# The last stage of an attention, mixture and gate chain in two passes, with seven block products in place of eight

## The chip, the cores and the metric

The kernel runs on one core of one Trainium2 chip. The metric is the device time of one execution in microseconds, as the median of several runs. A core has five engines that matter here, each with a queue of its own that it works through in order: TensorE (PE, matrix products into PSUM, with its weight loads listed as PEld), VectorE (DVE), ScalarE (ACT), GpSimd (POOL), and SyncE (SP), which here issues every DMA. An instruction starts when those ahead of it on its engine have started and its semaphore waits are met.

## The reference, cut to what matters

Three stages follow each other, for four batches of 576 tokens: an attention with 8 heads, a mixing layer (`_moe_ref`) and a gated layer, in which all of the change lies:

```python
def _moe2_ref(x, w_in, w_spatial, b_spatial, w_out):
    h = np.maximum(x @ w_in, 0.0)                # x: 4 x 576 x 512, w_in: 512 x 1024
    u, v = (h[..., :512], h[..., 512:])
    mu = np.mean(v, axis=-1, keepdims=True)
    var = np.mean((v - mu) ** 2, axis=-1, keepdims=True)
    v_n = (v - mu) / np.sqrt(var + 1e-06)
    v_s = np.einsum('ts,bsd->btd', w_spatial, v_n) + b_spatial[None, :, None]
    return ((u * v_s) @ w_out)                   # w_spatial: 576 x 576, w_out: 512 x 512
```

## The kernel before, in words

Everything is float32 at the interface. A product of two float32 matrices is made of three matmuls: each operand is split into a rounded high half and the remaining low half (names ending in h and l, or `_0` and `_1`), and hi·hi, hi·lo and lo·hi are added in PSUM. A split is a cast and a subtraction (`halves`, line 1342).

The instruction order is not the order of the source. Every step is handed to a planner (class `Plan`, line 185) by `add`, with the engines that could do it and an estimated cost; `Plan.order` then emits one list, by a list schedule whose priorities are the step's due time `plan.at` plus numbers from the table `TUNE` (line 57), one row per tag and kind of step. Where the planner expects PE to be idle, it inserts small matmuls of a constant into `psT`, whose result nobody reads. Since all instructions go through one helper, the profile knows them by line L500 alone; they are told apart by the tiles that they write and read.

The last stage (`moe2`, line 1737) is one pass per batch. It splits the batch's `x` into `x2h` and `x2l` (8 pieces of 288 columns); makes `vt`, the right half of the hidden layer, with tokens on partitions (4 tiles of 128 tokens, 12 matmuls of 512 columns each, into `psB`; the last 64 tokens of two batches share one more tile); normalises it on DVE (`BATCH_NORM_STATS2`, `mv`), splits it into `vh` and `vl`; makes `u`, the left half, with features on partitions; then the spatial product `sp`, the gate and the product with `w_out`. The products `u` and `sp` are the ones that the change rewrites. Each has 8 groups per batch, 4 blocks of 128 features by 2 halves of 288 tokens. A `u` group contracts over 4 chunks of 128 with 3 matmuls each, 12; an `sp` group over 4 chunks of tokens with 3 each and a chunk of the last 64 tokens (`vx`, hi and lo stacked) with 2, 14. All of them are 288 columns wide and write the three banks `psM`. Then ACT takes `u` out of PSUM with the relu; for `sp` DVE adds the bias (`g<-psM,bb`), DVE or POOL multiplies by `u`, DVE or ACT casts to `gh` and DVE or POOL subtracts for `gl`. The `w_out` product and its copy `ot` end the batch; the batches' steps overlap as the planner's due times (1000 apart) allow.

Of the kernel before, what the change touches and what calls it, by code (L numbers as in the profile page):

```python
# [9 lines left out]
F32 = mybir.dt.float32  # L10
# [8 lines left out]
P = 128  # L19
# [18 lines left out]
def blocks(dil):  # L38
# [473 lines left out]
def kernel(  # L512
# [51 lines left out]

    enter("all", "cp")
    enter("all", "psM", space=PSUM)
    enter("one", "w1")
    enter("one", "mp")
    enter("att", "ap", side="right")
    enter("att", "psS", space=PSUM)  # L570
# [44 lines left out]
    def chunk(key, x):  # L615

        k = (key, x)
        if k not in tiles:
            home, tag = key, x
            if key[0] in WHOLE and x == 1:  # L620
                home, tag = before(key), 2
# [1422 lines left out]
```

## Time and profile before

| | us |
|---|---|
| median of 3 runs | 571.61 (570.77 to 572.67) |
| the profiled execution | 567.52 |
| its span in the trace | 565.7 |
| PE busy | 553.6 |
| DVE busy | 344.3 |
| ACT busy | 257.0 |
| POOL busy | 88.4 |

The profiled execution's own time is 4.1 us under the median and 1.8 us over its span. The profile lists for each engine the time in which it worked, and follows the chain of work that ended last back from the end, each step to what released it. The granted TensorE clock is 1.00 in every stretch, the higher of the two levels (2.4 GHz). The last stage runs from about 348 us to the end.

### The profile page before, as it was taken

How to read it: one execution, taken by the hardware profiler on the slowest of the kernel's cores; microseconds unless marked ns; L12 is line 12 of the kernel's file. 1: busy time of each engine (PE TensorE's matmuls, PEld its weight loads, DVE VectorE, ACT ScalarE, POOL GpSimd, SP SyncE). 2: the span in 40 equal slices, each digit the busy share in tenths (PEclk: the TensorE clock that was granted, in tenths of full speed). 3: DMA queues.
4: the chain of work that ended last, by engine and by line, in shares of the span. 5: the costliest groups of instructions: out<-in, count | busy, mean ns of one | idle time of the engine just before them, and what ended most of it. 6: DMA issues, size and time to landing. Idle time of an engine off the chain costs nothing.

```text
span 565.7 us, 13681 instructions
## 1 busy us (share of the span) xinstructions
PE 553.6 (98%) x5755; PEld 501.2 (89%) x5766; DVE 344.3 (61%) x782; ACT 257.0 (45%) x575; POOL 88.4 (16%) x105
## 2 busy tenths in 40 slices
PE   9999999998999999999999999999999999999997
PEld 5567876798999999999999999989889889988996
DVE  1999857957986383956689322389326428745150
ACT  2779825435724636316557560485334033214222
POOL 0100014432631022001001021006311000000030
PEclk9999999999999999999999999999999999999999
DMA  9978984357356200002342100312100010010002
GB/s 206 235 229 288 189 128 80 57 138 126 59 100 137 44 1 3 1 1 69 102 127 99 42 27 1 96 37 76 47 29 1 1 64 30 1 39 37 1 1 93
DMA packets 96253, 43.08 MB, mean 76 GB/s; under 512 B 81536, under 2 KB 89216, under 8 KB 96192
## 3 DMA queue, kind: packets, MB, share of 16 engines
q1 hardware_dynamic: 96192, 42.21, 31.7%
q8 instruction: 45, 0.74, 0.6%
q14 instruction: 16, 0.13, 0.1%
HBM read 37.47 MB, written 4.72 MB: 75 GB/s over the span
## 4 chain that ended last, share of the span: by engine, by line
PE 87%; DVE 3%; DMA 3%; ACT 2%; SPq 2%; issue 1%; DVEq 0%; ACTq 0%
PE psM L500 60%; PE psB L500 18%; PE psT L500 6%; SPq L500 2%; PE psS L500 2%; DMA room<-in_moe_w_v_dram 1%; DMA vw<-in_v_dram 1%; DVE xm L500 1%; DMA ld<-in_k_dram 1%; DVE xl L500 1%; ACT xh L500 0%; DVE xh L500 0%; ACT room L500 0%; ACT xm L500 0%; ACT wv L500 0%
## 5 line engine op out<-in xcount | busy, mean ns | idle before, releaser
L500 PE MATMUL psM<-xh,wk 128*128 128x288 f32 (+2 forms) x512 | 119.1, 326 | 1.5 <-DVE x L500 0.7
L500 PE MATMUL psM<-sq_dt.float32r,wv 128*128 128x288 f32 (+2 forms) x768 | 113.8, 299 | 1.0 <-ACT wv L500 0.6
L500 PEld LDWEIGHTS psM<-sq_dt.float32r,wv 128*128 128x128 f32 x768 | 104.5, 188 | 3.2 <-ACT wv L500 0.8
L500 PEld LDWEIGHTS psM<-xh,wk 128*128 128x128 f32 x512 | 87.1, 188 | 8.6 <-ACT xh L500 0.9
L500 PE MATMUL psM<-xh,wr 128*128 128x288 f32 (+2 forms) x256 | 64.0, 327 | 0.6 <-DVE xh L500 0.6
L500 PE MATMUL psM<-xl,wk 128*128 128x288 f32 x192 | 56.5, 295 | 0.1
L500 PE MATMUL psM<-x2h,wi 128*128 128x288 f32 x256 | 54.8, 296 | 0.0
L500 PEld LDWEIGHTS psM<-xh,wr 128*128 128x128 f32 x256 | 44.5, 188 | 3.9 <-DVE xh L500 0.7
L500 DVE TENSOR_TENSOR sq_dt.float32r<-kr,sq_dt.float32r 128x288 fp32r<-128x288 f32 (+2 forms) x54 | 26.8, 502 | 26.3 <-ACT sq_dt.float32r L500 25.8
L500 PEld LDWEIGHTS psM<-x2h,wi 128*128 128x128 f32 x256 | 42.2, 188 | 0.6 <-ACT u L500 0.2
L500 PE MATMUL psB<-wo,gh 128*128 128x512 f32 (+1 forms) x136 | 40.3, 379 | 0.0
L500 PE MATMUL psB<-wi,x2h 128*128 128x512 f32 x128 | 40.2, 395 | 0.0
L500 PE MATMUL psM<-x2l,wi 128*128 128x288 f32 x128 | 37.8, 296 | 0.9 <-DVE x2l L500 0.9
L500 ACT ACTIVATE kr<-psM 128x288 f32<-128x288 f32 (+2 forms) x50 | 20.3, 410 | 40.3 <-PE psM L500 37.0
L500 PE MATMUL psM<-wsh,vh 128*128 128x288 f32 x128 | 38.1, 298 | 0.0
L500 PE MATMUL psM<-wsl,vh 128*128 128x288 f32 x128 | 37.7, 295 | 0.0
L500 PE MATMUL psM<-wsh,vl 128*128 128x288 f32 x128 | 37.7, 294 | 0.0
L500 PEld LDWEIGHTS psM<-xl,wk 128*128 128x128 f32 x192 | 36.1, 188 | 0.3 <-DVE xl L500 0.3
L500 POOL TENSOR_TENSOR xl<-xm,xh 128x288 fp32r<-128x288 f32 x18 | 15.6, 876 | 127.6 <-ACT xh L500 67.8
L500 DVE BATCH_NORM_STATS2 bn<-vt 128x6 f32<-128x512 f32 x18 | 12.4, 691 | 37.6 <-ACT vt L500 37.5
L500 DVE TENSOR_TENSOR g<-psM,bb 128x288 f32<-128x288 f32 x32 | 14.3, 455 | 28.6 <-PE psM L500 25.1
L500 DVE SCALAR_TENSOR_TENSOR x<-x,psM 128x288 f32<-128x288 f32 (+2 forms) x32 | 14.3, 452 | 28.0 <-PE psM L500 27.8
(160 smaller groups left out, 1102.8 us busy)
## 6 DMA issues: line engine op xcount, KB each, us to landing
vw<-in_v_dram SPq DMA_DIRECT2D x36, 128.0 KB, 3.4
room<-in_moe_w_k_dram SPq DMA_DIRECT2D x8, 512.0 KB, 7.2
room<-in_moe_w_v_dram SPq DMA_DIRECT2D x8, 512.0 KB, 5.3
raw<-in_moe_w_in_dram SPq DMA_DIRECT2D x8, 512.0 KB, 3.8
ld<-in_q_dram SPq DMA_DIRECT2D x48, 72.0 KB, 2.6
ld<-in_k_dram SPq DMA_DIRECT2D x48, 72.0 KB, 2.7
vw<-in_v_dram SPq DMA_DIRECT2D x8, 288.0 KB, 5.3
room<-in_moe_w_r_dram SPq DMA_DIRECT2D x4, 512.0 KB, 4.2
```

The source lines that it names most:

```text
L500: return self.tc.keep_in_program_order(getattr(self.engine, name)(*args, **kw))
```

## The change

`moe2` is split in two functions. `first_half(b)` is run for all four batches, then `second_half(b)` for all four. Between them the normalised `vt` tiles lie in a DRAM tile `vnd` (16 DMAs of 256 KB to it, 8 of 512 KB back into the two `raw2` buffers, which the weight loads use before); `u` stays in SBUF, written over the batch's `x`, and is now kept without the relu, which moves into the gate (`SCALAR_TENSOR_TENSOR`, max with 0, then multiply).

The products `u` and `sp` are cut into 2 by 2 blocks and made from seven block products instead of eight (`seven`). A block product has two quarters `q` of 128 features and contracts over 2 chunks, so it is 2·2·3 = 12 matmuls of 288 columns, and seven of them 84. For `sp` 16 matmuls for the last 64 tokens are added. Some products need sums of blocks as operands: for `u` sums of `w_in` blocks, made once (`stationary`, tiles `qw`), and sums of `x` blocks, per batch (`moving`, tiles `t`); for `sp` sums of blocks of the transposed `w_spatial`, made once (`wsq`), and sums of blocks of the normalised `v`, per batch (`stationary` again, tiles `qv`). Products 1, 6, 7 and 4 accumulate one after another in the same bank of a quarter (`psM_91` and `psM_92`, "A"); in between, `take` copies the bank's value into a tile `sn` (for `sp` with the bias). Products 2, 5 and 3 use `psM_100` and a fifth bank of `psB` ("B"), and `final` adds an `sn` tile to a bank.

With this, per kernel, u and sp matmuls go from 832 to 736; transposes of `w_spatial` from 25 to 30 (6 blocks of 96 rows); DVE has 790 instructions for 732, ACT 605 for 565, POOL 139 for 100, and 270 DMAs are issued for 244. The whole table `TUNE` has new numbers, so all stages are ordered anew. The core of the diff:

```diff
...
-    ('u', 0): {'psM': (-2395, 121810, 792, 22), 'u': (73178, 190977, 792, 2000)},
...
+    ('T', 0): {'part3': (159936, 0, 792, 800), 'part1': (-65152, 0, 200, 800), 'part2': (-312122, 0, 1500, -300), 't': (-25768, 30350, 0, 0), 'part4': (68946, 0, 792, 2000)},
...
+    def quarter(i, x, phase):
+        k = 2 * (i - 1) + x
+        return held("w1", [P, 2, HD], F32R, f"q{phase}{k}", old_tags["wk"][k])
+
+    def hl(src, hi, lo, n, src_keys, hk, lk, after=()):
+
+        add(
+            {"act": act(n), "dve": dve2(n)}, lambda e: copy(e, hi(), src()),
+            r=src_keys, w=[hk], two="both", after=after,
+        )
+        return len(plan.ops) - 1, add(
+            {"dve": dve(n), "pool": pool(n)},
+            lambda e: two(e, lo(), src(), f32(hi()), ALU.subtract),
+            r=list(src_keys) + [hk], w=[lk], two=True,
+        )
+
+    def combine(o, a, b_, op, n, r, w, after=()):
+        return add(
+            {"dve": dve(n), "pool": pool(n)}, lambda e: two(e, o(), a(), b_(), op),
+            r=r, w=w, two=True, after=after,
+        )
...
+    def stationary(a11, a12, a21, a22, keys, phase, first=()):
+
+        k11, k12, k21, k22 = keys
+        QW = 2 * HD
+
+        def both(i, src, ks):
+            return hl(
+                src, quarter(i, 0, phase), quarter(i, 1, phase), QW, [*ks, *first], ("q", i, 0), ("q", i, 1),
+            )
+
+        both(1, a11, k11)
+        d12 = both(2, a12, k12)
+        x1 = combine(s_[0], a21, a22, ALU.add, QW, [*k21, *k22], [("vt", 0)])
+        combine(s_[1], s_[0], a11, ALU.subtract, QW, [("vt", 0), *k11], [("vt", 1)])
+        both(6, s_[1], [("vt", 1)])
+        both(5, s_[0], [("vt", 0)])
+        combine(a21, a11, a21, ALU.subtract, QW, [*k11, *k21], [("a21",)], after={x1})
+        both(7, a21, [("a21",)])
+        both(4, a22, k22)
+        combine(a12, a12, s_[1], ALU.subtract, QW, [*k12, ("vt", 1)], [("a12",)], after=d12)
+        both(3, a12, [("a12",)])
+        return [("a21",), ("a12",)]
+
+    ended = stationary(wq[0, 0], wq[0, 1], wq[1, 0], wq[1, 1], [wkept] * 4, "w", ["q room"])
...
+    def moving(b11, b12, b21, b22, keys, readers, split_, name):
+
+        k11, k12, k21, k22 = keys
+        QW = 2 * HALF
+        a3 = combine(b22, b22, b12, ALU.subtract, QW, [*k22, *k12], [(name, 3)], after=readers[3])
+        a1 = combine(b12, b12, b11, ALU.subtract, QW, [*k12, *k11], [(name, 1)], after={a3, *readers[1]})
+        combine(b11, b22, b11, ALU.add, QW, [(name, 3), *k11], [(name, 2)], after={a1, *readers[0]})
+        split_(6, b11, [(name, 2)])
+        split_(5, b12, [(name, 1)])
+        split_(7, b22, [(name, 3)])
+        combine(b21, b21, b11, ALU.subtract, QW, [(name, 2), *k21], [(name, 4)], after=readers[2])
+
...
+    def seven(name, b, at, left, right, tails, bias, final):
+
+            ps, key = bank_of(where, q)
+            n = 2 + (tail is not None)
+            for z in range(n):
+                last = z == n - 1
+
+                def emit(e, z=z, last=last):
+                    o = ps()[:, :HALF]
+                    fresh = start and z == 0
+                    flags = {} if start and stop else {"skip_group_check": True}
+                    if z == 2:
+                        nc.tensor.matmul(o, lh(), rh(), start=False, stop=False, **flags)
+                        nc.tensor.matmul(o, lh(), rl(), start=False, stop=True, **flags)
+                    nc.tensor.matmul(o, lh, rh, start=fresh, stop=False, **flags)
+                    nc.tensor.matmul(o, lh, rl, start=False, stop=False, **flags)
+                    nc.tensor.matmul(o, ll, rh, start=False, stop=last, **flags)
+
...
+        def take(ps, key, h):
+            t, tk = snap()
+            if bias is None:
+                add(
+                    {"act": actp(HALF), "dve": dve(HALF)}, lambda e: copy(e, t(), ps()[:, :HALF]),
+                    r=[key, "p2"], w=[tk],
+                )
+            else:
+                add(
+                    {"dve": dve(HALF)}, lambda e: two(e, t(), ps()[:, :HALF], bias(h), ALU.add),
+                    r=[key, "p2", "bb"], w=[tk],
+                )
+            return t, tk
+        qs = range(2)
+        for q in qs:
+            ps, key = run(1, q, "A")
+            t1 = take(ps, key, 0)
+            ps, key = run(2, q, "B", tail=tail(q, 0))
+            final(q, 0, ps, key, t1)
+        t2_, t3_, c_ = {}, {}, {}
+        for q in qs:
+            t2_[q] = take(*run(6, q, "A", False), 1)
+        right.late()
+        for q in qs:
+            c_[q] = run(5, q, "B")
+        for q in qs:
+            t3_[q] = take(*run(7, q, "A", False, tail=tail(q + 2, 1)), 1)
+            final(q + 2, 1, *c_[q], t3_[q])
+        for q in qs:
+            final(q + 2, 0, *run(4, q, "A", False, tail=tail(q + 2, 2)), None)
+        for q in qs:
+            final(q, 1, *run(3, q, "B", False, tail=tail(q, 1)), t2_[q])
+
...
+        def final(o, h, ps, key, t):
+            u = lambda: xs[b][:, o, h * HALF : (h + 1) * HALF]
+            area = users_of([(("T", b), ((2, 1), (4, 3))[o // 2][h])])
+            w = [("u", b, o, h)]
+            if t is None:
+                add({"act": actp(HALF), "dve": dve(HALF)}, lambda e: copy(e, u(), ps()[:, :HALF]), r=[key], w=w, after=area)
+            else:
+                add(
+                    {"dve": dve(HALF)}, lambda e: two(e, u(), ps()[:, :HALF], t[0](), ALU.add),
+                    r=[key, t[1]], w=w, after=area,
                 )
...
+    def second_half(b, base):
...
+        for j in range(2):
+            dma2(
+                packets(2 * P, 2048), vn[j],
+                lambda j=j: vnd[b, 2 * j * P : 2 * (j + 1) * P].rearrange("(a p) n -> p a n", p=P),
+                r=[("vnd", b, t) for t in (2 * j, 2 * j + 1)], w=[("vn", j), ("a21",) if j == 0 else ("a12",)],
+                after=raw_done,
+            )
...
+        def final(o, h, ps, key, t):
+            gk = plan.slot("g2", 6)
+            g = t2([P, HALF], F32, f"g{gk}", f"t{gk // 2}{gk % 2}")
+            hs = slice(h * HALF, (h + 1) * HALF)
+            add(
+                {"dve": dve(HALF)},
+                lambda e: two(e, g(), ps()[:, :HALF], t[0]() if t else bb()[:, hs], ALU.add),
+                r=[key, t[1] if t else "bb"], w=[("g2", gk)], after=t_done,
+            )
+            add(
+                {"dve": dve(HALF)},
+                lambda e: nc.vector.scalar_tensor_tensor(
+                    g(), xs[b][:, o, hs], 0.0, g(), op0=ALU.max, op1=ALU.mult
+                ),
+                r=[("g2", gk), ("u", b, o, h)], w=[("g2", gk)], two=True,
+            )
+            hl(
+                g, lambda: gh()[:, o, hs], lambda: gl()[:, o, hs], HALF,
+                [("g2", gk)], ("gh", o, h), ("gl", o, h), after=x_done,
...
     for b in range(B):
-        moe2(b, 10000 + 1000 * b)
+        first_half(b, 9200 + 600 * b)
+    for b in range(B):
+        second_half(b, 12000 + 600 * b)
```

Three places of the order. The first is ACT where the last stage begins, before: the gate inputs of the last mixing half (`x_1045`), then the eight casts of batch 0 into `x2h`.

```order
L500 ACTIVATE x_1045<-psM_92 128x288
L500 ACTIVATE x_1045<-psM_100 128x288
L500 ACTIVATE x_1045<-psM_91 128x288 x2
L500 CAST x2h<-x_120 128x288 x8
L500 ACTIVATE u<-psM_100 128x288
L500 ACTIVATE u<-psM_92 128x288
L500 ACTIVATE u<-psM_91 128x288
```

And now; `x_1053` is the last mixing half's tile, `wide` receives the transposed `w_spatial`.

```order
L558 ACTIVATE x_1053<-psM_91 128x288
L558 ACTIVATE wide<-psB_4191 128x4x96
L558 ACTIVATE wide<-psB_4284 128x4x96
L558 ACTIVATE wide<-psB_4365 128x4x96
L558 CAST x2h<-x_123 128x2x288 x3
L558 ACTIVATE wth<-psB_4365 128x96
L558 CAST wsq_0_4689<-wide 128x576
```

On ACT the casts were eight of 288 columns directly behind those of the mixing layer. Now there are three of 2x288, behind three copies for `wide`; the fourth is on DVE. DVE there before, with the last gate steps of the mixing layer:

```order
L500 SCALAR_TENSOR_TENSOR x_1045<-x_1045,psM_92 128x288
L500 SCALAR_TENSOR_TENSOR x_1045<-x_1045,psM_100 128x288
L500 SCALAR_TENSOR_TENSOR x_1045<-x_1045,psM_91 128x288
L500 SCALAR_TENSOR_TENSOR x_1045<-x_1045,psM_92 128x288
L500 MEMSET eps 128x1
L500 TENSOR_TENSOR x2l<-x_120,x2h 128x288 x2
L500 MEMSET zero 128x1
```

And now:

```order
L558 SCALAR_TENSOR_TENSOR x_1053<-x_1053,psM_92 128x288
L558 SCALAR_TENSOR_TENSOR x_1053<-x_1053,psM_100 128x288
L558 SCALAR_TENSOR_TENSOR x_1053<-x_1053,psM_91 128x288
L558 SCALAR_TENSOR_TENSOR x_1053<-x_1053,psM_92 128x288
L558 CAST x2h<-x_123 128x2x288
L558 TENSOR_TENSOR x2l<-x_123,x2h 128x2x288 x4
L558 TENSOR_TENSOR wsq_1_4712<-wide,wsq_0_4689 128x576
```

The four gate steps were followed by `x2l` of 288 columns (with one small memset between); now they are followed by a cast and `x2l` subtractions of twice the width.

The second place is PE in a spatial product. Before, three groups took turns in `psM`, here with matmuls of `vt` between:

```order
L500 MATMUL psM_100<-wsh,vh 128x288
L500 MATMUL psM_100<-wsl,vh 128x288
L500 MATMUL psM_100<-wsh,vl 128x288
L500 MATMUL psM_92<-wsh,vh 128x288
L500 MATMUL psM_92<-wsl,vh 128x288
L500 MATMUL psM_92<-wsh,vl 128x288
L500 MATMUL psB_4767<-wi_512_0_4183,x2h 128x512
L500 MATMUL psB_4767<-wi_512_1_4194,x2h 128x512
```

Now product 6 of the first batch (first rows) is followed in the same bank, `psM_91`, by product 7, six matmuls later:

```order
L558 MATMUL psM_91<-wsq_0_5016,qv_5670 128x288
L558 MATMUL psM_91<-wsq_1_5030,qv_5670 128x288
L558 MATMUL psM_91<-wsq_0_5016,qv_5683 128x288
L558 MATMUL psM_92<-wsq_0_5016,qv_5670 128x288
L558 MATMUL psM_92<-wsq_1_5030,qv_5670 128x288
L558 MATMUL psM_92<-wsq_0_5016,qv_5683 128x288
L558 MATMUL psB_4721<-wsq_0_4987,qv_5631 128x288
L558 MATMUL psB_4721<-wsq_1_4997,qv_5631 128x288
L558 MATMUL psB_4721<-wsq_0_4987,qv_5649 128x288
L558 MATMUL psM_91<-wsq_0_4961,qv_5638 128x288
L558 MATMUL psM_91<-wsq_1_4968,qv_5638 128x288
L558 MATMUL psM_91<-wsq_0_4961,qv_5664 128x288
```

In between the value of `psM_91` has to be taken out. Before, a bank that was full was written again by a new group, after at least five or six matmuls into other banks.

The third place is SP's queue. Before, all that follows the loads of `w_out` is output:

```order
L500 DMA raw_0_3860<-in_moe_w_out_dram 128x1024
L500 DMA out_dram<-ot_5184 128x512
L500 DMA out_dram<-ot_5193 128x512
L500 DMA out_dram<-tmp_0_3925 128x512
L500 DMA out_dram<-tmp_1_3944 128x512
L500 DMA out_dram<-ot_5193 128x512
L500 DMA out_dram<-tmp_0_3925 128x512
```

Now the reads of `vnd` (`raw<-vnd`) stand between the outputs:

```order
L558 DMA raw_0_3745<-vnd 128x2x512
L558 DMA raw_1_3731<-vnd 128x2x512
L558 DMA raw_0_3745<-vnd 128x2x512
L558 DMA out_dram<-ot_5881 128x512
L558 DMA raw_1_3731<-vnd 128x2x512
L558 DMA out_dram<-ot_5910 128x512
L558 DMA out_dram<-ot_5934 128x512
L558 DMA out_dram<-ot_5968 128x512
L558 DMA raw_0_3745<-vnd 128x2x512
L558 DMA raw_1_3731<-vnd 128x2x512
```

An output behind a read is issued only when the read's wait, for the last reader of its buffer, is over.

## Rows read from the trace of the kernel before

**Rows 1.** The page: busy time (us, share, count), then the chain that ended last.

```profile
PE 553.6 (98%) x5755; PEld 501.2 (89%) x5766; DVE 344.3 (61%) x782; ACT 257.0 (45%) x575; POOL 88.4 (16%) x105
...
PE 87%; DVE 3%; DMA 3%; ACT 2%; SPq 2%; issue 1%; DVEq 0%; ACTq 0%
```

**Rows 2.** Windows by stretch: length, then busy us of PE, PEld, DVE, ACT, POOL; clock.

```profile
0.00:45.00 45.00, 41.18 (x599) 27.59 (x607) 31.42 (x79) 26.79 (x54) 3.27 (x12) 1.00 0.94 231
45.00:200.00 155.00, 150.86 (x2304) 133.32 (x2306) 115.31 (x239) 84.74 (x198) 40.28 (x44) 1.00 0.61 117
200.00:345.00 145.00, 144.91 (x1534) 143.26 (x1533) 89.06 (x217) 71.17 (x164) 16.56 (x20) 1.00 0.15 46
345.00:355.00 10.00, 9.14 (x71) 8.90 (x69) 2.95 (x9) 1.43 (x4) 0.00 (x0) 1.00 0.00 0
355.00:500.00 145.00, 145.00 (x886) 131.85 (x885) 85.93 (x197) 54.77 (x120) 21.30 (x20) 1.00 0.12 37
500.00:562.60 62.60, 62.51 (x372) 56.30 (x370) 19.66 (x44) 17.83 (x38) 6.96 (x9) 1.00 0.10 36
```

**Rows 3.** The chain in order of time, last stage: start, us, what (count).

```profile
419.48 14.23 PE psM L500 x107
...
521.05 18.30 PE psM L500 x138
...
549.42 13.11 PE psB L500 x69
...
562.55 0.37 ACT ot L500
```

**Rows 4.** Groups by shape from 348 us: duration min/median/max in ns, first and last start.

```profile
L500 PE MATMUL psM<-x2l,wi x128: 290/295/399, 349.0 to 538.9; 128*128 128x288 f32 x128
...
L500 PE MATMUL psM<-wsh,vl x128: 289/294/300, 376.6 to 548.9; 128*128 128x288 f32 x128
```

**Rows 5.** The same view, DVE, ACT and POOL.

```profile
L500 DVE TENSOR_TENSOR g<-psM,bb x32: 443/458/460, 386.3 to 549.5; 128x288 f32<-128x288 f32 x32
...
L500 DVE TENSOR_TENSOR gl<-g,gh x23: 445/459/1275, 389.4 to 501.6; 128x288 fp32r<-128x288 f32 x23
...
L500 POOL TENSOR_TENSOR gl<-g,gh x9: 803/810/982, 437.1 to 551.4; 128x288 fp32r<-128x288 f32 x9
...
L500 ACT CAST vh<-vt x12: 610/620/630, 374.3 to 524.0; 128x512 fp32r<-128x512 f32 x12
L500 DVE TENSOR_TENSOR vl<-vt,vh x11: 658/683/693, 375.3 to 524.7; 128x512 fp32r<-128x512 f32 x11
L500 POOL TENSOR_TENSOR vl<-vt,vh x5: 1298/1300/1364, 397.8 to 475.7; 128x512 fp32r<-128x512 f32 x5
```

**Rows 6.** Timeline where the last stage begins: start, us, what [idle before].

```profile
347.80 0.29 PE L500 MATMUL psM<-x2h,wi 128*128 128x288 f32 x1
348.07 0.46 DVE L500 SCALAR_TENSOR_TENSOR x<-x,psM 128x288 f32<-128x288 f32 x1 [2.38 <-PE psM L500]
348.45 0.45 DVE L500 TENSOR_TENSOR x2l<-x,x2h 128x288 fp32r<-128x288 f32 x1
...
348.95 0.40 PE L500 MATMUL psM<-x2l,wi 128*128 128x288 f32 x1 [0.86 <-DVE x2l L500]
```

**Rows 7.** Window of 20 us in which POOL is busiest; columns as in Rows 2.

```profile
380.00:400.00 20.00, 20.00 (x131) 18.67 (x130) 17.77 (x33) 9.82 (x19) 12.34 (x11) 1.00 0.16 54
```

**Rows 8.** Groups of DVE in 380 to 400 us: count, busy us, mean ns.

```profile
L500 DVE TENSOR_TENSOR gl<-g,gh 128x288 fp32r<-128x288 f32 x6 | 4.6, 797 | 0.5 <-ACT gh L500 0.5
...
L500 DVE TENSOR_TENSOR g<-psM,bb 128x288 f32<-128x288 f32 x7 | 3.1, 455 | 0.6 <-PE psM L500 0.3
L500 DVE CAST gh<-g 128x288 fp32r<-128x288 f32 x3 | 2.0, 706 | 0.7 <-POOL g L500 0.7
```

**Rows 9.** DMA issues of the page: count, KB each, us from issue to landing.

```profile
raw<-in_moe_w_in_dram SPq DMA_DIRECT2D x8, 512.0 KB, 3.8
...
out_dram<-tmp SPq DMA_DIRECT2D x8, 256.0 KB, 2.0
```

More of the change, by code (lines that the diff above doesn't have):

```diff
@@ L640, in behind, with split_weight @@
         return [loads[k] for k in follows.get((b, qd, what), ())]
-    def split_weight(pool_name, src, rows, cols, name, raw_of, nraw, tmp_of, ntmp, order, step=0, lead=0, room=()):
+    def split_weight(pool_name, src, rows, cols, name, raw_of, nraw, tmp_of, ntmp, order, step=0, lead=0, room=(), kept=None):
         s = src.bitcast(U32).rearrange("(r p) c -> p r c", p=P)
@@ L653, in split_weight, with number @@
             pool_of[name] = pool_name
-            if whole:
+            keep = kept is not None and c0 == 0
+            if keep:
+                tk = ("kept", r)
+                def number(r=r):
+                    return kept(r)
+            elif whole:
                 tk = ("whole", key)
@@ L707, in split_weight @@
             add({"dve": dve(CH)}, lower, r=[tk, rk, yk], w=[tk], two=True)
-            if not whole:
+            if not whole and not keep:
                 split(key, number, tk, room)
@@ L1620, in open_w2, with held, tile_, nothing @@
         enter("two", "psB", space=PSUM, reuse_waits="tile")
+    def held(pool_name, shape, dtype, name, tag=None):
+        def tile_():
+            if name not in tiles:
+                tiles[name] = pools[pool_name].tile(shape, dtype, tag=tag or name, name=name)
+            return tiles[name]
+        return tile_
+    def nothing(e):
+        pass
+    HD = DM // 2
     plan.at = 4905
@@ L1628, with room @@
         lambda i: get("w2", [P, CH], F32, f"tmp2_{i}"), ("tmp2", 2), ["w2"],
+        kept=lambda r: wideb()[:, r, :CH],
     )
+    old_tags = {
+        nm: [tag_of((nm, r, c0), x)[1] for c0 in range(0, cols, CH) for r in range(NC) for x in range(2)]
+        for nm, cols in (("wk", DF), ("wr", DM))
+    }
+    for r in range(NC):
+        shared["wo", r, 0] = ("wr", r, 0)
+    def room(name, old, cols):
+        plan.tag = ("p2",)
+        add(
+            {}, nothing, w=[name], lat=0,
+            after=users_of([((old, r, c0), x) for c0 in range(0, cols, CH) for r in range(NC) for x in range(2)]),
+        )
@@ new lines @@
+    combine(d, lambda: f32(wth()[:, h0]), lambda: f32(wth()[:, h1]), ALU.subtract, HALF, tl, [dk])
+    combine(d, d, lambda: f32(wtl()[:, h0]), ALU.add, HALF, [*tl, dk], [dk])
+    combine(d, d, lambda: f32(wtl()[:, h1]), ALU.subtract, HALF, [*tl, dk], [dk])
+    add({"act": act(HALF), "dve": dve2(HALF)}, lambda e: copy(e, wdh(), d()), r=[dk, "q room"], w=["wdh"], two="both")
+    combine(
+        lambda: wdl()[:LR], lambda: d()[:LR], lambda: f32(wdh()[:LR]), ALU.subtract, HALF, [dk, "wdh"], ["wdl"],
+    )
@@ new lines @@
+    add(
+        {"dve": dve(HALF)},
+        lambda e: nc.vector.tensor_copy(wdl()[LR:], zero()[LR:].to_broadcast([LR, HALF])),
+        r=["zero", "q room"], w=["wdlz"],
+    )
+    dma2(packets(P, 2304), bb, b_sp.partition_broadcast(P), r=["p2"], w=["bb0"])
+    add(
+        {"act": act(S), "dve": dve2(S)},
+        lambda e: nc.scalar.mul(bb(), bb(), 0.5) if e == "act" else nc.vector.tensor_scalar(bb(), bb(), 0.5, None, op0=ALU.mult),
+        r=["bb0"], w=["bb0", "bb"], two="both",
+    )
@@ L1750, in moe2 @@
[L1750 to L1761 removed]
+                after=users_of([("vtmp",)]) if b else (),
+            ))
@@ new lines, in first_half @@
+        plan.at = base
+        for h in range(2):
+            for j in range(2):
+                hs = slice(h * HALF, (h + 1) * HALF)
+                readers[2 * j + h] |= set(hl(
+                    xq[j][h],
+                    lambda j=j, hs=hs: xh()[:, 2 * j : 2 * j + 2, hs],
+                    lambda j=j, hs=hs: xl()[:, 2 * j : 2 * j + 2, hs],
+                    2 * HALF, xk[j][h] + ["p2"], ("x2h", j, h), ("x2l", j, h),
+                ))
+                if h:
+                    readers[2 * j + h] |= uses[b]
@@ L1762, in moe2 @@
+        for t in list(range(NT)) + ([NT] if not even else []):
+            plan.at = base + 40 * t
             plan.tag = ("vt", b if t < NT else "e%d" % b)
-            ps, key = bigbank()
+            pair = b // 2
+            ps, key = slots4()
             def tok(a, e, c, t=t):
@@ L1833, in moe2 @@
+            add(
+                {"act": act(DM), "dve": dve2(DM)},
+                lambda e, vt=vt, tmp=tmp: copy(e, tmp(), vt()),
+                r=[("vt", vk)], w=[("vtmp",)], two="both", after=users_of([("eh", 0), ("eh", 1)]),
+            )
+            for d in range(2):
+                rows = slice(d * LR, (d + 1) * LR)
+                x = 2 * pair + d
                 add(
                     {"act": act(DM), "dve": dve2(DM)},
-                    lambda e, vt=vt, tmp=tmp: copy(e, tmp(), vt()),
@@ new lines, in left, with right, right_keys @@
+        def left(i, x, q, z):
+            return quarter(i, x, "w")()[:, z, q * P : (q + 1) * P]
+        XB = {1: (0, 0), 2: (1, 0), 3: (1, 1)}
+        def right(i, x, z):
+            if i < 4:
+                j, h = XB[i]
+                return (xh, xl)[x]()[:, 2 * j + z, h * HALF : (h + 1) * HALF]
+            return ttile(i, x)()[:, z]
+        def right_keys(i):
+            if i < 4:
+                return [("x2h", *XB[i]), ("x2l", *XB[i])]
+            return [("t", TS[i], x) for x in range(2)]
@@ L1996 @@
             plan.ops[i][1](e)
-    for g in ("three", "two", "all"):
+    for g in ("three", "two", "w1", "all"):
         stacks[g].close()
```

492 lines of the change are left out of this document (285 added, 207 removed), and 244 rows, old and new, of the table TUNE.

## The prediction

> **What bounds the kernel now.** I read the page's busy time first: PE works 553.6 of 565.7 us and 87% of the chain that ended last is PE; DVE works 61% of the span, POOL 16% [rows 1]. The windows by stretch then show where the other 12.1 us are: 45.00 − 41.18 = 3.8 before 45 us, 155.00 − 150.86 = 4.1 to 200 us, 0.1 to 345 us, 0.9 between 345 and 355 us, none from 355 to 500 us, and after the last matmul at 562.5 some 3.2 us for one copy and its output [rows 2, 3]. So the last stage, which the change rewrites, is PE from end to end, with one wait of 0.86 us at its start [rows 6]. Time goes away there only with PE work, and comes back wherever another engine then no longer keeps up.
>
> **The change part by part.**
>
> Removed, products. Per batch `u` falls from 8·12 = 96 matmuls to 7·12 = 84 and `sp` from 8·14 = 112 to 84 + 16 = 100; over four batches 832 becomes 736, 96 fewer, all of 288 columns and of the kinds in [rows 4]. Their 0.29 us each is pipelined; the chain has a piece of 138 of them in 18.30 us and one of 107 in 14.23 [rows 3], 0.1326 and 0.1330 us apiece. At 96·0.1326 that is **−12.7 us**, all of it on PE's path. Matmuls that accumulate into the same bank stand close together in both kernels, so I take the same pace. The five more transposes (30 of 96 rows for 25) have about 75% of the columns of the old; I put them at **+0.1**.
>
> Moved, start of the stage. Before, one `x2h` matmul ran at 347.80, then PE waited for the last gate step on DVE (348.07, 0.46 us, which needs the last mixing group) and for `x2l` behind it, to 348.95 [rows 6]. Now the cast for the first `x2l` stands behind that gate step too, and cast and subtraction are 576 wide. From the pace of the 288 and 512 wide rows (0.45 and 0.68 us, [rows 5]) the subtraction is about 0.75 instead of 0.45, and the cast, which was finished early, adds some 0.4. That would be 0.7 more; PE has `x2h` work of its own now for part of it, or ACT's casts come later still (three copies for `wide` are ahead of them). I take **+0.7**, range 0.2 to 1.2.
>
> Added, work beside PE in the first pass. The sums `t` of `x` blocks, their casts, the split of `wsq` and the copies of `sn` are new, and the saving removes the PE time that hides them. Counting the order of the changed kernel from its first `x2h` matmul to the end of the first pass with the durations of [rows 5], scaled by width, gives PE 94 us, DVE 75, ACT 51, POOL 35 (23 of its 26 operations at 1.3 to 1.5 us). In the second pass it is PE 88, DVE 50, ACT 27, POOL 39. No single engine passes PE, in no piece of some 15 us by more than 0.3 us for DVE alone. But DVE and POOL are not independent. The window with most POOL work has DVE busy 17.77 us and POOL 12.34 of 20, with PE full [rows 7]; there the six `gl` subtractions took 797 ns on average where 459 is the median, and three casts 706 where the `g<-psM,bb` adds stayed at 455 [rows 5, 8]. That is 6·0.34 + 3·0.4 = 3.2 us lengthened in two forms; with the rest of the window some 4 us, a third of POOL's 12.34. So part of POOL's time, for operations with two SBUF inputs and for casts, is DVE's loss. With half of POOL's time added to DVE, the pieces with most of both (21 us of PE against 16.9 DVE and 8.7 POOL; 17.5 against 15.9 and 5.6) pass PE by 0.3 and 1.2 us, and in a row by up to 3.7; with a third they hardly do. I take **+1.2**, range 0 to 3.7.
>
> Here the Trainium skill speaks against the change: "SBUF — State Buffer", section "Who interferes with whom", has the port pair that DVE and GpSimd share as an exclusive lock, on which the loser blocks for a whole instruction. The lengthened `gl` rows agree with it; how much of DVE's work comes under it is what decides. Taken for all of it, the sum would be rival C's, 576 to 591 us, in place of mine.
>
> Added, turnarounds of a PSUM bank. Products 1, 6, 7 and 4 follow each other in one bank, and a copy to `sn` has to come between; counted in the order, some 30 of these have only six to eight matmuls beside them, 0.80 to 1.06 us. What a turnaround needs can be read at the start of the stage: the last matmul before the wait gave way to the next at 347.80, DVE started at 348.07, took 0.46, and PE started 0.05 us after the `x2l` behind it ended [rows 6]: 0.27 + 0.46 + 0.05 = 0.78 us, if DVE is free just then. That is no room. On the other hand the old order has some 40 turnarounds of five or six matmuls too, most through ACT, several in the 107 matmuls from 419.48 on, and the chain goes through them without a wait [rows 3]. With DVE at 57 to 80% of PE's time instead of ACT, a few will be late by part of an operation of 0.45. I take **+0.5**, range 0 to 3.5 (30 waits of a quarter of an operation).
>
> Added, the way through DRAM. A 256 KB write lands in 2.0 us and a 512 KB read in 3.8 [rows 9]. For batch 0 the reads can start as soon as its `vt` tiles are written, tens of microseconds ahead. For batches 1 to 3 they wait until the sums of the batch before have been read out of `raw2`, then come 3.8 us and 8 split steps on DVE, ACT and POOL (POOL's at 1.3 us); a pass has 84 us for four such rounds, 21 each, of which this takes about 3.8 + 8 = 12. It is hidden unless POOL falls behind. I take **+0.5**, range 0 to 3.8, one uncovered read. Outputs queued behind a read on SP wait a little, but four `ot` tiles cover that.
>
> Moved, the first 348 us. Nothing but the order and two or three idle-time matmuls more. The stretches before 200 us lose 7.9 us now [rows 2], so there is room for either sign: **+0.7**, range −0.8 to 2.2, since the first loads carry more small steps ahead of them in the new order.
>
> Moved, the tail. Before, 13.1 us of `w_out` matmuls followed the last spatial product [rows 3]. Now some 5.6 us do, and the last product's chain (add, gate, cast, subtraction: four steps of 0.3 to 0.46, 1.7 us with their handovers) has some 2 us of PE beside it: **+0.2**, range 0 to 1.
>
> Sum: −12.7 + 0.1 + 0.7 + 1.2 + 0.5 + 0.5 + 0.7 + 0.2 = **−8.8 us**. The profiled execution of 567.5 would become 558.7. It lies 4.1 us under the median of the runs shown; with the same distance the median is 571.6 − 8.8 = **562.8 us**.
>
> **The rivals.**
>
> A, full saving: the planner's order holds, nothing but the start gives anything back. −12.6 + 0.7 = −11.9, **559.7 us**; −0.8 at the front would make it 558.9. For it: 145 us in a row without any PE wait [rows 2]. Against it: the window of [rows 7] was the only one of its kind, and now two thirds of the pass is like it.
>
> B, most of it is given back by turnarounds and POOL together: 3.5 + 3.7 + 0.7 + 2 = 9.9 of 12.6, **569 us**. For it: the 0.78 us against 0.80. Against: the old turnarounds that cost nothing.
>
> C, slower: DVE and POOL shut each other out completely. Then 75 + 35 = 110 us stand against 94 of PE in the first pass, 16 us, and 50 + 39 = 89 against 88 in the second, 1 us, and more where pieces are uneven, up to 32 in all when each piece is taken alone: 571.6 − 12.6 + 17 to 32, **576 to 591 us**. It decides from about 0.7 of POOL's time lost to DVE (11 us given back). For it: single `gl` subtractions of 1275 ns. Against: 17.77 + 12.34 = 30 us in a window of 20 without a wait of PE, even if 4 us of it is waiting [rows 7, 8], and DVE's 30 us in the first pass that read PSUM or statistics with one SBUF input, such as the 455 ns adds.
>
> D, the change doesn't do what it says, for instance since more idle-time matmuls or lost first-stage order cost as much as is saved: near **571 us**.
>
> **How the numbers follow.** Forecast 0.55 (560.5 to 566), A 0.16, B 0.14, C 0.08, D 0.07. The predicted time is 562.8. The range leaves C and D out, and the outer part of A and B: 557.5 to 570. What this measurement can tell from no change is about 0.3%, 1.7 us, so faster means under 569.9: forecast, A and most of B, 0.83; same 0.08; slower 0.09.
>
> **What would show it.** PE busy falls by 11 to 13 us, to about 541, and PE's idle time in the last stage rises from 0.9 to 2 to 5 us. The start's wait is 1.2 to 2 us. The `psM` waits, if any, name DVE or ACT `sn` copies (turnarounds), `t` or `x2l` (POOL and DVE), or `qv` (DRAM); the `raw<-vnd` reads land in about 4 us. The forecast is wrong if PE's pace in the products differs from 0.1326, if DVE's two-input operations are lengthened throughout the first pass, or if the stretch before 345 us changes by over 2 us.

## The result

The changed kernel took 564.02 us (median of 4 executions, 561.33 to 566.17) beside 571.77 us of the kernel before (4, 570.77 to 572.67): a ratio of 0.9863, interval 0.9816 to 0.9909. Two later comparisons gave 560.26 us against 570.36 (0.9839, 0.9799 to 0.9879) and 562.40 against 570.95 (0.9831, 0.9802 to 0.9859). The prediction was 562.8, with −8.8 us; the three medians are 7.8, 10.1 and 8.6 us under before. Medians and ratios below leave out one execution of `extra_product` (580.50 us) and one of `warm_4` (882.31 us, at a mean granted clock of 0.557), which were over 1.5% above the fastest of their kernel.

The profiled execution of after was its slowest, 566.17 us (span 564.4), so its two halves have to be read apart. First the page, busy times, and then the windows of [rows 2] again (length, then PE, PEld, DVE, ACT, POOL, granted clock):

```profile
PE 551.7 (98%) x5677; PEld 492.0 (87%) x5677; DVE 390.9 (69%) x840; ACT 278.6 (49%) x615; POOL 144.5 (26%) x144
...
PE 78%; DMA 6%; SPq 5%; DVE 4%; ACT 3%; issue 2%; POOL 0%; DVEq 0%; POOLq 0%
```

```profile
0.00:45.00 45.00, 42.77 (x586) 26.27 (x587) 26.61 (x66) 22.66 (x42) 5.02 (x14) 0.89 0.87 196
45.00:200.00 155.00, 150.36 (x2181) 130.90 (x2180) 119.46 (x261) 83.17 (x197) 30.05 (x34) 1.00 0.66 127
200.00:345.00 145.00, 144.49 (x1626) 141.51 (x1625) 83.50 (x191) 74.39 (x176) 32.07 (x37) 1.00 0.17 50
```

The granted clock is 0.89 in the first 45 us, where before it was 1.00 [rows 2]. Finer windows show where: at full clock to 25 us, then

```profile
25.00:30.00 5.00, 3.98 (x107) 3.03 (x103) 1.94 (x6) 1.93 (x6) 0.19 (x1) 0.65 1.10 211
30.00:35.00 5.00, 5.00 (x25) 3.30 (x22) 4.61 (x13) 3.41 (x8) 0.00 (x0) 0.50 0.98 272
35.00:40.00 5.00, 5.00 (x80) 2.46 (x81) 2.13 (x7) 1.00 (x3) 0.00 (x0) 0.83 0.29 102
```

0.50 is the lower level, 1.2 GHz. Just ahead of the fall TensorE had run small matmuls of `pt` and then waited (the timeline; what it waited for stands in brackets):

```profile
26.39 0.99 PE L558 MATMUL psM<-ident,early 16*128 16x16 f32 x8 [1.02 <-DMA early<-in_q_dram]
```

In this execution the last stage begins 10 us later than in the profile of before. But the last stage itself is much shorter. The same span in the profile of before and in two profiles of after, from the first `x2h` matmul to the last `ot` copy:

```profile
347.80:562.55 214.75, 213.85 (x1303) 194.26 (x1301) 108.09 (x248) 73.98 (x161) 28.26 (x29) 1.00 0.11 35
```

```profile
358.75:561.33 202.58, 201.12 (x1190) 180.59 (x1190) 156.52 (x315) 95.60 (x196) 77.33 (x59) 1.00 0.23 75
```

```profile
352.92:555.22 202.30, 200.80 (x1190) 180.49 (x1190) 156.40 (x315) 95.68 (x196) 77.28 (x59) 1.00 0.22 76
```

So between these marks the stage is 12.2 and 12.4 us shorter, and what differs between the two profiles of after lies ahead of it: it begins at 358.75 us in one and 352.92 in the other. The marks favour the change a little, since before the first `x2h` matmul ran ahead of the start's wait and now it runs behind a part of it. Counted from the end of the last mixing product (347.97 us before, 358.00 and 352.18 in the two profiles) the stage is 11.2 and 11.5 us shorter. TensorE's waits in it, of the second profile (total, times, longest):

```profile
PE psM L558 <- DVE sn L558: 1.0, 2, 0.7
PE psM L558 <- ACT x2h L558: 0.8, 1, 0.8
PE psM L558 <- DVE x2l L558: 0.5, 1, 0.5
```

The last two are the start of the stage. In the chain of the first profile it reads, beside [rows 6]:

```profile
358.00 0.03 issue
...
358.10 0.45 DVE x L558
358.55 0.37 DVE x2h L558
358.92 0.68 DVE x2l L558
...
359.64 2.51 PE psM L558 x17
```

From the end of the last mixing product to the first `x2l` product it is 1.64 us (358.00 to 359.64) where it was 0.98 (347.97 to 348.95).

### The profile page after: what moved, and what is told of

Same layout as the page of the kernel before. It is cut to its first block, busy times and chain, and to the rows that moved or that the text cites. A ratio compares the mean times of both kernels' runs of the same rounds, so it can differ in the third digit from the quotient of the medians.

```text
span 564.4 us, 13784 instructions
## 1 busy us (share of the span) xinstructions
PE 551.7 (98%) x5677; PEld 492.0 (87%) x5677; DVE 390.9 (69%) x840; ACT 278.6 (49%) x615; POOL 144.5 (26%) x144
## 4 chain that ended last, share of the span: by engine, by line
PE 78%; DMA 6%; SPq 5%; DVE 4%; ACT 3%; issue 2%; POOL 0%; DVEq 0%; POOLq 0%
PE psM L558 50%; PE psB L558 22%; SPq L558 5%; PE psT L558 4%; PE psS L558 2%; DMA ld<-in_k_dram 2%; DMA early<-in_q_dram 2%; DMA vw<-in_v_dram 1%; DMA room<-in_moe_w_v_dram 1%; DMA room<-in_moe_w_r_dram 1%; ACT xh L558 0%; ACT xm L558 0%; ACT kr L558 0%; POOL xl L558 0%; DVE xh L558 0%
## 5 line engine op out<-in xcount | busy, mean ns | idle before, releaser
L558 PE MATMUL psM<-wsq,qv 128*128 128x288 f32 x264 | 41.8, 298 | 0.9 <-DVE sn L558 0.9
L558 PEld LDWEIGHTS psM<-wsq,qv 128*128 128x128 f32 x264 | 37.3, 188 | 2.7 <-DVE sn L558 1.6
L558 POOL TENSOR_TENSOR pr<-pr,st 128x384 f32<-128x384 f32 (+1 forms) x17 | 15.3, 906 | 72.3 <-DVE st L558 68.9
L558 DVE SCALAR_TENSOR_TENSOR xm<-x,mu,xm 128x288 f32<-128x288 f32 x48 | 25.3, 539 | 8.3 <-ACT xm L558 7.9
L558 DVE TENSOR_TENSOR sq_dt.float32r<-kr,sq_dt.float32r 128x288 fp32r<-128x288 f32 (+2 forms) x47 | 21.7, 466 | 11.0 <-ACT sq_dt.float32r L558 10.7
L558 ACT CAST sq_dt.float32r<-kr 128x288 fp32r<-128x288 f32 (+1 forms) x47 | 20.5, 436 | 17.0 <-POOL kr L558 10.1
L558 PE MATMUL psM<-xl,wr 128*128 128x288 f32 x96 | 28.2, 294 | 0.0
L558 PEld LDWEIGHTS psB<-wo,gh 128*128 128x128 f32 x136 | 24.5, 188 | 4.0
L558 ACT COPY ot<-psB 128x512 f32<-128x512 f32 (+1 forms) x19 | 10.7, 565 | 33.6 <-PE psB L558 30.3
L558 PEld LDWEIGHTS psB<-wi,x2h 128*128 128x128 f32 x128 | 23.0, 188 | 4.3
```

The lines of the kernel that those rows point to most:

```text
L558: return self.tc.keep_in_program_order(getattr(self.engine, name)(*args, **kw))
```

## The experiments

**What the saved products are worth.** `extra_product` puts 96 matmuls back:

```diff
+                    for _ in range(2 if i == 2 and fresh else 0):
+                        nc.tensor.matmul(o, lh, rh, start=True, stop=True)
+                        nc.tensor.matmul(o, lh, rl, start=True, stop=True)
+                        nc.tensor.matmul(o, ll, rh, start=True, stop=True)
```

> The changed kernel with the 96 matmuls put back: product 2 starts its bank twice more, 6 discarded matmuls of 288 columns ahead of each of its 16 runs, nothing else in the order. If the saving is PE time at 0.1326 us each and all of it on the path: the last stage is 203.3 + 12.7 less the waits that it now covers (about 1) = 215 us, and the time is within 3 us of the kernel before. Rival (a part of the gain is the two-pass form itself, fewer waits or cheaper evictions): the last stage stays under 212 us and the time 4 us or more under before.

```profile
354.69:569.19 214.50, 213.15 (x1286) 193.08 (x1286) 154.59 (x315) 95.64 (x196) 76.50 (x59) 1.00 0.21 71
```

The stage is 214.50 us, 12.2 more than 202.3, 0.127 us for each matmul, and the kernel is at 573.11 us against 570.30 (ratio 1.0046, 1.0012 to 1.0080). So the two passes and the sums alone win nothing and cost some 3 us: the gain is the 96 matmuls.

**What POOL costs.** `thin_pool` cuts POOL's subtractions and sums for the later batches to 16 columns, `double_pool` issues those twice that don't overwrite their own input; the order stays. Each of the two has one execution.

```diff
+    def thin(slim, e, o, a, b, op):
+        if slim and e == "pool":
+            o, a, b = (t[:, :16] if len(t.shape) == 2 else t[:, :, :8] for t in (o, a, b))
+        two(e, o, a, b, op)
```

```diff
+    def twice(e, o, a, b, op):
+        for _ in range(2 if e == "pool" and o is not a and o is not b else 1):
+            two(e, o(), a(), b(), op)
```

> The changed kernel with the POOL operations on x blocks of batches 1 to 3, on v sums of batches 2 and 3 and on gl shortened to 16 columns (the rest of their outputs keeps old values, so that part is left out); order and waits are the same. If POOL's hold on DVE cost PE the 0.9 us of waits for sn in the second pass: these waits fall to under 0.2 us, DVE's busy time in the last stage falls by 8 to 15 us, and the stage is 0.7 to 1 us shorter (202.3). Rival (the bank turnaround alone is too short): the waits for sn stay at 0.9.

> The changed kernel with each POOL subtraction and sum of the last stage that does not overwrite its own input issued twice, same order. If DVE loses a fifth to a half of POOL's time and had room: DVE's busy time rises by 8 to 25 us, the stage by 1 to 8 us. Rival (full exclusion, rival C of the prediction): the stage grows by 15 us or more. If POOL is without weight: under 0.5 us.

The stage of `thin_pool`, then of `double_pool` with TensorE's waits in it:

```profile
352.53:553.66 201.13, 200.56 (x1190) 180.61 (x1190) 143.04 (x315) 95.53 (x196) 37.74 (x59) 1.00 0.22 76
```

```profile
355.98:590.33 234.35, 211.54 (x1190) 185.63 (x1190) 177.66 (x315) 95.37 (x196) 133.72 (x102) 0.97 0.19 65
...
PE psM L558 <- POOL t L558: 8.5, 3, 3.7
PE psB L558 <- DVE g L558: 4.0, 4, 1.3
PE psM L558 <- POOL qv L558: 3.1, 1, 3.1
```

With 39.5 us less of POOL, DVE's busy time falls by 13.4 (156.4 to 143.0), a third, and the waits for `sn` are gone; the stage is 1.2 us shorter. All of that is in the second pass, as the two passes of `after_again` and then of `thin_pool` show, split at the same place of the order:

```profile
352.92:450.90 97.98, 97.47 (x565) 86.44 (x566) 87.23 (x175) 60.76 (x128) 35.90 (x27) 1.00 0.23 79
450.90:555.22 104.32, 103.33 (x628) 94.05 (x626) 69.17 (x141) 34.92 (x69) 41.38 (x33) 1.00 0.21 72
```

```profile
352.53:450.50 97.97, 97.46 (x565) 86.44 (x566) 81.87 (x175) 60.65 (x128) 20.13 (x27) 1.00 0.23 79
450.50:553.66 103.16, 103.10 (x627) 94.16 (x626) 61.18 (x141) 34.87 (x69) 17.61 (x33) 1.00 0.22 73
```

With 56 us more of POOL, DVE rises by 21 (0.38 of it) and the stage by 32. That is far over the 1 to 8 us expected, and by its length alone it would pass for the rival, full exclusion; what speaks against the rival is the 0.38. Of the 32 us, 21 are waits of TensorE and 11 its own busy time, to which the clock adds: behind three single waits of 3.1 to 3.7 us, and once behind several short ones, the granted clock was at 0.50 for some 3.4 us, here behind the wait for `qv` (the second line is a window of 1 us with TensorE's busy time and the clock):

```profile
474.08 1.57 PE L558 MATMUL psM<-wsq,qv 128*128 128x288 f32 x7 [3.11 <-POOL qv L558]
...
475.00:476.00 1.00, 1.00 (x6) 0.50 0.00 0
```

Both of POOL's ways are in the second waits: it is late itself (`t`, `qv`), and it makes DVE late. What a third means can be seen in the subtractions `gl<-g,gh` of DVE, min/median/max in ns, of after and of `thin_pool`:

```profile
L558 DVE TENSOR_TENSOR gl<-g,gh x24: 441/454/1533, 464.3 to 557.1; 128x288 fp32r<-128x288 f32 x24
```

```profile
L558 DVE TENSOR_TENSOR gl<-g,gh x24: 446/457/468, 458.1 to 549.5; 128x288 fp32r<-128x288 f32 x24
```

A subtraction that met a POOL sum took up to 1.53 us; with short POOL operations none took over 0.47. This agrees with the Trainium skill, "SBUF — State Buffer", section "Who interferes with whom", that the loser of the shared port blocks for a whole instruction. It is a third and not all, since POOL often runs while DVE waits, reads PSUM or runs statistics: beside the same POOL work no `sn` addition with one input in PSUM took over 0.46 us, and no statistics step over 0.70 for a median of 0.69.

```profile
L558 DVE TENSOR_TENSOR sn<-psM,bb x24: 441/458/459, 456.6 to 543.1; 128x288 f32<-128x288 f32 x24
...
L558 DVE BATCH_NORM_STATS2 bn<-vt x18: 662/685/695, 368.8 to 450.0; 128x6 f32<-128x512 f32 x18
```

**Where the wait for `sn` comes from.** The place in the timeline of after:

```profile
504.64 2.12 DVE L558 TENSOR_TENSOR gl<-g,gh 128x288 fp32r<-128x288 f32 x2
...
505.14 1.29 POOL L558 TENSOR_TENSOR vt<-raw,raw 128x512 f32<-128x512 f32 x1 [1.23 <-DMA raw<-vnd]
...
506.68 0.81 DVE L558 TENSOR_TENSOR sn<-psM,bb 128x288 f32<-128x288 f32 x2
...
507.54 1.07 PE L558 MATMUL psM<-wsq,qv 128*128 128x288 f32 x6 [0.68 <-DVE sn L558]
```

Two `gl` subtractions, one held beside a POOL sum, stand ahead of the copies that free bank A. `sn_first` exchanges them:

```diff
+    late = [s for s in steps if s[0] in (2706, 2629)]
+    steps = [s for s in steps if s[0] not in (2706, 2629)]
+    k = [i for i, _ in steps].index(2722) + 1
+    steps[k:k] = late
```

> The changed kernel with two steps of DVE's order exchanged in the second pass: the two gl subtractions that stood ahead of two sn copies near 505 us (one of them held for 1.5 us beside a POOL sum) stand behind them. If the 0.7 us wait of TensorE there is a copy late behind a subtraction that POOL holds up: the wait goes, the last stage is 201.4 to 201.8 us for 202.3, the time as the changed kernel's or a little under it (the difference is less than it can tell). If the bank's turnaround itself or the products ahead are the cause: the wait stays at 0.7 us.

```profile
359.16:562.15 202.99, 201.23 (x1190) 180.72 (x1190) 156.24 (x315) 95.73 (x197) 77.51 (x59) 1.00 0.22 75
...
PE psM L558 <- DVE g L558: 0.8, 1, 0.8
...
PE psM L558 <- DVE sn L558: 0.4, 1, 0.4
```

A miss: the stage is 0.7 us longer, not shorter. The wait moved to the `g` step behind the exchanged subtractions, which took 2.12 us there too. So DVE as a whole is behind at that place, and which step is late follows the order; only less held-up work (`thin_pool`) took the wait away. The median was 561.08 against 569.81.

**The way through DRAM.** `double_read` (one execution) issues each read of `vnd` twice.

```diff
-        add({"dma": cost}, lambda e: nc.sync.dma_start(o(), i() if callable(i) else i), r=r, w=w, lat=2000, after=after)
+        def go(e):
+            for _ in range(times):
+                nc.sync.dma_start(o(), i() if callable(i) else i)
```

> The changed kernel with each of the 8 reads of the normalised v from DRAM issued twice in a row, the second over the first. If the way through DRAM is hidden, as the prediction has it but for 0.5 us: the last stage stays at 202.3 us within 0.5. Rival (the reads of batches 1 to 3 come just in time): each of three rounds is late by up to the 2 to 4 us that a second read takes, the stage grows by 2 to 10 us.

```profile
354.71:571.98 217.27, 204.82 (x1190) 181.54 (x1190) 159.22 (x315) 95.54 (x197) 77.78 (x59) 0.99 0.26 90
```

The stage grows by 15.0 us, more than either expectation. The second read starts when the first has landed, so each of the four rounds is some 4 us later. Of the 15.0 us, 11.0 are waits of TensorE and 4.0 its own busy time; a part of these 4.0 is the clock, which was at 0.50 for 3.4 us behind a wait of 3.6 us near 467. Two things are late. In the rounds of batches 1 to 3 the splits of the next `v` wait for the read. And in the first pass the reads of batch 0 hold SP's queue while writes stand behind them; the chain of this kernel:

```profile
392.68 4.38 DMA raw<-vnd
...
397.48 4.49 DMA vnd<-vt
...
402.00 0.61 ACT vt L558
```

The `vt` buffer is free only when its write is out, so ACT's next `vt` is late, and TensorE with it. In the changed kernel itself a read lands in 3.9 us and no TensorE wait names a read or `qv`: the way through DRAM is hidden, but with well under 4 us a round to spare.

**The stretch ahead of the last stage.** Seven runs bear on it. `after_again` and `after_third` are the changed kernel itself. `front_before` has the priorities of before for the attention and mixing steps, with the new last stage; `front_after` those of after, with the old last stage. The edit is an exchange of rows of `TUNE`, here one that goes out in `front_after`:

```diff
 TUNE = {
...
-    ('k', 0, 0): {'xh': (-24563, 236971, 200, 800), 'psM': (-174639, -500052, 792, 22), 'kr': (161808, 224958, 200, 2000), 'kh': (-54256, -141643, -200, 300), 'kl': (40360, 347679, 200, 800)},
```

> The changed kernel as it is, for more executions with their clock. In its profile the last stage begins at 358.0 us where it began at 348.0 before, and it is 11.3 us shorter (203.3 for 214.6 us). Theory 1 (the front is slow because of its order and of a drop of the granted clock near 27 us, which does not fall in the same way each time): spans differ by execution with the clock, 559 to 565 us, the ones at clock 1.00 about 4 to 5 us shorter. Rival (the front is longer by work of the last stage that was moved into it): spans agree within 1 us, whatever the clock.

> The changed kernel with the priorities of the kernel before for the attention and mixing steps; the order of the first 590 steps on TensorE is then word for word that of before, the last stage is still the new one in two passes. Theory 1 (the 10 us are the new order of the front): the last stage begins near 348 to 350 us, the span is 553 to 557, the time 9 to 13 us under before. Rival (they come from last-stage work in the front, which is still there): the last stage begins near 356 to 358, the time is 5 to 8 us under before.

> The kernel before with the priorities of the changed kernel for the attention and mixing steps only; the last stage is the old one. Theory 1: the last stage begins near 353 to 358 us and the time is 3 to 9 us over before. Rival: it begins near 348 to 350 and the time is within 2 us of before.

`warm_gap` and `warm_4` add 8 or 4 matmuls of a constant ahead of the transposes that waited at 26 us; `head_spliced` issues the first 700 steps in the order of before. The edits (for `warm_4` the 8 is a 4; `spliced` puts the list of before's first 700 steps ahead of the rest):

```diff
+            if pe_at == 58:
+                for _ in range(8):
+                    nc.tensor.matmul(
+                        get("psT", [P, 512], F32, "psT2"), ones[:, :P], wide_ones, start=True, stop=True
+                    )
...
-    for i, e in plan.order():
+    for i, e in spliced(plan.order()):
```

> The changed kernel with 8 more matmuls of a constant on TensorE just ahead of the transposes that waited 1.0 us for the early query load at 26.4 us, behind which the granted clock was at its lower level (1.2 GHz) for 10.2 us. If the small matmuls and the wait there are what makes the clock fall: the clock is 1.00 in the front, the last stage begins some 4 us earlier (354), the time is 2 to 5 us under the changed kernel. Rival (the clock falls for what happens earlier, or is of no weight): within 1 us of the changed kernel.

> As warm_gap with 4 matmuls for 8. If 8 were enough to keep the clock up but cost time themselves where the load was not late: clock at 0.997 or above in most executions and the time 0 to 2 us under the changed kernel (558 to 560). If fewer don't hold the clock: spans spread from 556 to 564 as in the changed kernel.

> The changed kernel with the first 700 steps (to just ahead of the second batch's mixing products) issued in the order of the kernel before, the rest in its own order. Between two traces with the same early loads these steps took 1.6 us longer in the new order (first product of the second batch at 124.4 for 122.8 us). If the order of the head is that loss: the last stage begins 1 to 2 us earlier than in the changed kernel, the time is 1 to 3 us under it (557 to 560), and 2% or more under before. Rival (the head differs by when the early loads land, not by its order): the same as the changed kernel within 1 us.

> The changed kernel once more beside the two others: 558 to 566 us by the clock and the landing of the early loads; the last stage again 202.3 us within 0.3.

| kernel | median us | before beside it | spans of single executions at clock 0.999 or 1.00 | at lower mean clock |
|---|---|---|---|---|
| after (three series) | 564.02, 560.26, 562.40 | 571.77, 570.36, 570.95 | 556.4, 557.8, 557.8, 559.3, 559.6 | 558.3 to 564.4 |
| front_before | 568.89 | 570.36 | none | 565.4 to 571.5 |
| front_after | 571.83 | 570.36 | 567.5 to 571.2 | 569.4 to 575.1 |
| warm_gap | 562.12 | 570.36 | 558.9 to 561.2 | none |
| warm_4 | 561.69 | 570.30 | 558.9 to 562.8 | 562.4, and 880.5 at 0.557 |
| head_spliced | 563.99 | 570.95 | 558.3, 558.3 | 561.8 to 563.2 |

Before itself has spans of 565.3 to 569.1 at full clock, and up to 572.7 at 0.994. At equal clock after is about 9.5 us shorter (median span 557.8 of 5 executions for 567.35 of 24). So the lower clock is no loss that the change brought; it falls on both. With more matmuls at that place it stayed at 0.999 or 1.00 in 9 of 11 executions, as the first theory said; of the two others one had 0.991 and one 0.557, at 880.5 us, which nothing here explains. But the time did not fall: these 9 executions are no faster than those of the changed kernel at full clock. That the added matmuls and the late load take the gain back is likely and not shown.

What differs at full clock can be followed by two marks, the first `xh,wk` product and the first `xl,wk` product, of before, after, `after_again` and `warm_4`:

```profile
L500 PE MATMUL psM<-xh,wk x512: 288/295/497, 28.9 to 330.3; 128*128 128x288 f32 x128, 128*128 128x256 f32 x22, 128*128 128x320 f32 x21
L500 PE MATMUL psM<-xl,wk x192: 290/294/396, 122.8 to 330.2; 128*128 128x288 f32 x192
```

```profile
L558 PE MATMUL psM<-xh,wk x512: 288/295/793, 32.4 to 340.2; 128*128 128x288 f32 x128, 128*128 128x256 f32 x22, 128*128 128x320 f32 x21
L558 PE MATMUL psM<-xl,wk x192: 290/294/402, 129.4 to 340.1; 128*128 128x288 f32 x192
```

```profile
L558 PE MATMUL psM<-xl,wk x192: 290/294/396, 124.4 to 334.3; 128*128 128x288 f32 x192
```

```profile
L558 PE MATMUL psM<-xl,wk x192: 290/294/398, 128.7 to 338.7; 128*128 128x288 f32 x192
```

The second mark stands at 122.8, 129.4, 124.4 and 128.7 us: `warm_4`, at full clock all the way, is nearly as late as after with 10 us of low clock. From there to the last stage's first `x2h` product it is 225.0 us before (122.8 to 347.8) and 228.5 to 229.4 in the other three. So the first 125 us vary by 5 us, with the landing of the early loads and with the clock, and the next stretch is 3.5 to 4.4 us longer. Of this 0.76 is the wait for `x2h` ahead of the first product, and 2.1 are transposes of `w_spatial`. Before, they ran from 354.5 us on, inside the stage; in `after_again` they begin at 304.5:

```profile
L500 PE MATMUL psB<-ident,raw x25: 222/272/273, 354.5 to 369.8; 128*128 128x128 f32 x20, 64*128 64x64 f32 x5
...
L558 PE MATMUL psB<-ident,raw x30: 243/246/302, 304.5 to 373.2; 96*128 96x96 f32 x30
```

Ten of them run inside the stage and take 1.2 us of TensorE there, the other 20 take 2.1 ahead of it; before, all 25 took 3.5 inside it.

`front_before` fell short of both expectations: with the old priorities the new last-stage work in the mixing steps (`wi`, `tmp`) meets DVE there, and TensorE waits 5.6 us at once:

```profile
PE psM L558 <- DVE xl L558: 5.6, 1, 5.6
```

So that run doesn't isolate the old front; `front_after` does, and has a ratio of 1.0029 (1.0001 to 1.0058), 1.5 us. Its last stage begins at 349.8 us, as its rival said, and not at 353 to 358. At equal clock the other way to the same figure is −9.5 + 12.4 − 0.76 − 2.1 = 0.0 us. So the new order of the front costs between nothing and 1.5 us. `head_spliced` shows no gain from the old head alone; its last stage began at 357.81 us, with 6.8 us of low clock in the profile.

## Why the prediction was right

| step | predicted us | shown |
|---|---|---|
| 96 matmuls fewer | −12.7 | −12.2 (`extra_product`) |
| transposes | +0.1 | −0.2 in sum; 2.1 moved ahead of the stage |
| start of the stage | +0.7 | +0.66 (1.64 for 0.98) |
| DVE beside POOL | +1.2 | together +1.2 (`thin_pool`), all in the second pass |
| bank turnarounds | +0.5 | no wait left once POOL is short |
| DRAM | +0.5 | 0, but no room |
| the first stretch | +0.7 | 0 to 1.5, beside the transposes |
| tail | +0.2 | 0 |

The product term was right in size and place: its pace was 0.127 instead of 0.1326. The start was right to 0.1 us. DVE beside POOL was the term that I gave the widest range with the turnarounds, and a third of POOL's time as DVE's loss, read off one window, is what `thin_pool` and `double_pool` showed (0.34 and 0.38). That the term came out at its 1.2 us is partly luck. I had expected it in the first pass, where `after_again` and `thin_pool` take 97.98 and 97.97 us; it is in the second. The count behind it was short as well: 94 us of TensorE and 75 of DVE in the first pass, 88 and 50 in the second, where the profile has 97.5 and 87.2, then 103.3 and 69.2. A third of POOL's time explains DVE's excess in the first pass, not all of it in the second; and 94 and 88 don't add up to the some 205 us that the forecast itself leaves for the stage.

Rival C, complete exclusion, is out, since it needed 0.7; but `double_pool` shows how near the point is: 73% more POOL time gives back all and more (595 us). Rival B's turnarounds cost nothing by themselves: some 30 at 0.80 to 1.06 us pass without a wait in `thin_pool`, as the old ones did. Rival A, 559.7 us, lies 0.6 us under the lowest of the three medians, and its −11.9 us is more than any of the three; the 1.2 us that POOL costs stand against it.

One step was wrong, though it didn't count: the room of the way through DRAM. I had put a round at 12 of 21 us and thought only a slow POOL could uncover it. `double_read` has 11.0 us of waits for four rounds of one more read, where by that count some 16 of 21 us a round would still have been hidden. The step that failed is the count of what stands behind a read: only the outputs on SP, it said, while the writes of `vnd` stand there too, and ACT's `vt` behind those.

The front was near the upper end of its range (at equal clock −9.5 + 12.4 − 0.76 = 2.1 us for −0.8 to 2.2), but for a reason that I hadn't listed: 2.1 us of transposes moved into it from the stage, which are the stage's gain there and no loss. So the two parts, stage and front, were each off and made up for each other: all terms but the front's came to −9.5 us, and the stage with its start is 11.2 to 11.5 us shorter, some 9 without the moved transposes.

Two of the signs that I named spoke against me. TensorE's busy time fell by 13.0 us in the stage, but in the whole page only to 551.7, and to 547.3 in `after_again`, not to 541: the front took the transposes, had stretches of low clock, and the page of before lacks at least 11 matmuls (5755 for 5766 weight loads). And the last stage begins 5.1 and 11.0 us later in the two profiles, past the 2 us that I gave as a sign of being wrong; with the clock, the early loads, the start's wait and the transposes counted off, nothing to 1.5 us is left. Beside that, the time of single executions moves by 8 us with the early loads and the clock, more than all terms but the first. About 1.6 us of TensorE's time in the stage have no name: its busy time fell by 13.0 us where 12.35 for the products (213.15 − 200.80) and some 2.3 for the transposes make 14.6.

## What to carry to other kernels

Where one engine works without a break, removing its instructions is worth their pace in the chain, and the question is only what was hidden beside them: sum the other engines' work against the shortened stretch, and count a part of POOL's time to DVE as well when both work on SBUF (here 0.34 to 0.38 of it). Test a hidden transfer by doubling it before calling it hidden with room. Compare a stage by its own length between two marks in the trace; here that was steady to 0.3 us where whole executions moved by 8.

## What had not been expected of the hardware

More than half of the executions of either kernel have a mean granted clock under 0.999. In the profiles of the changed kernel the clock is at its lower level for 3 to 10 us, twice near 27 and once near 60 us, so the place differs from one execution to the next, and executions at 0.994 are about 3 us longer than those at 1.00. Four or eight small matmuls more went with a clock of 0.999 or 1.00 in 9 of 11 executions and made the kernel no faster: that the lower clock goes together with late loads is a guess that no run here separates.
